# An attention-plus-MLP kernel on one core: the next item's first products ahead of the last item's third and fourth

## The chip, the cores and the metric

The kernel runs on one core of a Trainium2 chip. Time is device microseconds (us) of one execution; lower is better. The kernel before ran three times for its time and once more under the profiler. Engines are named as in the profile: PE (TensorE matmul), PEld (its weight load), DVE (VectorE), ACT (ScalarE), POOL (GpSimd), SP (SyncE).

## The reference

```
def _attn_ref(q, k, v, tau):                  # q, k, v: (2, 6016, 256)
    qn = q / (np.linalg.norm(q, axis=1, keepdims=True) + 1e-06)
    kn = k / (np.linalg.norm(k, axis=1, keepdims=True) + 1e-06)
    s = kn.transpose(0, 2, 1) @ qn / tau      # 256 x 256 per batch
    s = s - s.max(-1, keepdims=True)
    a = np.exp(s)
    a /= a.sum(-1, keepdims=True) + 1e-09
    return v @ a
def _moe_ref(x, w_in, w_out, alpha):          # x: (12032, 256), w_in: 256 x 2048
    h = x @ w_in
    g = np.maximum(h, 0.0) + alpha * np.minimum(h, 0.0)
    return g @ w_out
```

## The kernel before

The attention matrix is small, so the kernel folds it into the first weight: M = a @ w_in per batch. What is left per token is g = prelu(v @ M) and out = g @ w_out. The 12032 tokens are cut into 24 tiles of 500 or 504 tokens, twelve per batch, and the 2048 hidden units into eight pairs of 256. One tile and one pair make an *item*; item i has tile t = i // 8 and pair j = i % 8, and there are 192. Every float32 product is made in three passes of split operands (high by high, high by low, low by high), so one "product" below is three PE instructions at lines L115 to L117.

The first layer of an item is done with seven half-width products and additions between them (a Strassen-Winograd scheme). `pe_a` makes two products into the PSUM tile `q` (tag in the trace: q), which ACT copies out in `copies` (L605 into r0, L606 into p7). `pe_b` adds two products onto r0. `add_p7(i, 0)` on DVE (L622) makes the first half of r1 from r0 and p7. `pe_c` adds the third and fourth products, one onto that half of r1 and one onto r0. `add_p7(i, 1)` (L622 again) makes the other half of r1, and only then may `pe_d` add the last product onto r0. The activation takes two steps for each half: `act_n` on ACT (L635) and `dve_g` on DVE (L644), for r1 (n = 1) first, then r0 (n = 0).

The second layer has two forms. In most tiles, and for odd j in all of them, `g_high` (ACT, L653) and `g_low` (DVE, L657) split g, and twelve full-width products follow. In tiles 13 to 22 (`S_TILES`), even j is done by a second Strassen-Winograd scheme: `g_sums` (DVE, L694 to L699) makes sums t of g; `x_high` (ACT, L704) and `x_low` (DVE, L708) split g, `t_low` (ACT L717 and a POOL transfer L718) and `t_high` (ACT, L722) split t. Their products go to four PSUM banks X; `s2_first` runs three iterations after the item began and `s2_second` four. When a tile is through, `combine` (ACT L786, DVE L787 to L793) and two `finish_out` (DVE L800, then a transfer) empty the banks. `s_weights` makes four sets of summed weights on POOL (L680 to L686) with one ACT cast (L685) in each.

Each engine works through its own queue in the order in which the code issues. The order is written out by hand in one loop, `for i in range(NI + LAG)`: in iteration i the first layer of item i begins (`pe_a`, `pe_b`), that of item i-1 ends (`pe_c`, `pe_d`, activation), item i-2 is split, and the second layer of items i-3 and i-4 runs. At an iteration's end stands side work from a table (`side`): the preparation of the next tile's v in `v_sums`, `v_high`, `v_low` by the numbers `when`, and `s_weights`. `early` and `late` hold the two `finish_out` and `combine`: `combine` at the end of the iteration with j = 2, `finish_out` in the one with j = 3.

From tile 12 on r1 has one PSUM buffer (`r1_tile(..., alone=True)`), r0 has two, q has one.

Of the kernel before, what the change touches and what calls it, by code (L numbers as in the profile page):

```python
# [25 lines left out]
def fused_kernel(  # L26
# [67 lines left out]
    def f32(ap):  # L94
        return ap.bitcast(F32)
# [3 lines left out]
    def r1_tile(shape, name, alone=False):  # L99
        if alone or r1_at[0] % 2 == 0:  # L100
            r1_at[0] = 1
            return ps_r1.tile(shape, F32, tag="r1", name=name)
        r1_at[0] = 0
        return ps_x.tile(shape, F32, tag="x", name=name)
# [475 lines left out]
    def half_of(i):  # L580
        return tiles[items[i][0]][2] // 2

    def prod(out, i, p, first):
        t, j = items[i]
        h = half_of(i)
        m, v = M[tiles[t][0], j], v_spl[t]
        passes(
            out[:, :h], m[:, 0, p], m[:, 1, p], v[:, 0, p, :h], v[:, 1, p, :h],
            first, True, shared=True,
        )  # L590
# [6 lines left out]
    def copies(i):  # L597
        h = half_of(i)
        x = q_t.pop(i)
        r_t[i] = [  # L600
            ps_r.tile([P, 2, HW_], F32, tag="r0", name=f"r0_{i}"),
            r1_tile([P, 2, HW_], f"r1_{i}", alone=items[i][0] >= S_TILES[0] - 1),
        ]
        p7_t[i] = p7pool.tile([P, HW_], F32, tag="p7", name=f"p7_{i}")
        nc.scalar.copy(r_t[i][0][:, :, :h], x[:, 0:1, :h].broadcast_to([P, 2, h]))  # L605
        nc.scalar.copy(p7_t[i][:, :h], x[:, 1, :h])  # L606

    def pe_b(i):
        prod(r_t[i][0][:, 0], i, 1, False)
        prod(r_t[i][0][:, 1], i, 5, False)  # L610

    def pe_c(i):
        prod(r_t[i][1][:, 0], i, 3, False)
        prod(r_t[i][0][:, 1], i, 4, False)

    def pe_d(i):
        prod(r_t[i][0][:, 1], i, 2, False)

    def add_p7(i, n):
        h = half_of(i)  # L620
        r = r_t[i]
        nc.vector.tensor_tensor(  # L622
            out=r[1][:, n, :h], in0=r[0][:, 1, :h], in1=p7_t[i][:, :h], op=ALU.add
        )

    def blocks(x, i, a, b):
        h = half_of(i)
        return x[:, a * h : b * h].rearrange("p (n c) -> p n c", n=b - a)
# [11 lines left out]
    def dve_g(i, fi):  # L640

        f = 2 * items[i][1] + fi
        g = blocks(g_t[i], i, 2 * fi, 2 * fi + 2)
        nc.vector.scalar_tensor_tensor(  # L644
            out=g, in0=r_t[i][fi][:, :, : half_of(i)], scalar=sgn[:, f : f + 1],
            in1=g, op0=ALU.mult, op1=ALU.max,
        )

    def g_high(i, fi):
        w = tiles[items[i][0]][2]  # L650
        if fi == 1:
            gs_t[i] = [gpool.tile([P, 2, TW], F32R, tag=x, name=f"{x}{i}") for x in ("gh", "gl")]
        nc.scalar.copy(gs_t[i][0][:, fi, :w], g_t[i][:, fi * w : fi * w + w])  # L653

    def g_low(i, fi):
        w = tiles[items[i][0]][2]
        nc.vector.tensor_tensor(  # L657
            out=gs_t[i][1][:, fi, :w], in0=g_t[i][:, fi * w : fi * w + w],
            in1=f32(gs_t[i][0][:, fi, :w]), op=ALU.subtract,
        )  # L660
# [5 lines left out]
    def in_s(i):  # L666
        return 0 <= i < NI and items[i][0] in S_TILES

    def is_s(i):
        return in_s(i) and items[i][1] in S_J  # L670
# [30 lines left out]
    def x_high(i):  # L701
        h = half_of(i)
        xs_t[i] = [raw.tile([P, 2 * TW], F32R, tag="raw", name=f"{x}{i}") for x in ("xh", "xl")]
        nc.scalar.copy(xs_t[i][0][:, h : 4 * h], g_t[i][:, h : 4 * h])  # L704
# [8 lines left out]
    def t_low(i):  # L713

        w = 4 * half_of(i)
        ts_t[i] = [gpool.tile([P, 2 * TW], F32R, tag=x, name=f"t{x}{i}") for x in ("gh", "gl")]
        nc.scalar.activation(ts_t[i][1][:, :w], tt_t[i][:, :w], AF.Copy, scale=-1.0)  # L717
        nc.gpsimd.dma_start(out=ts_t[i][1][:, :w], in_=tt_t[i][:, :w], accum_op=ALU.add)  # L718
# [87 lines left out]
    def stage2(i):  # L806

        t, j = items[i]
        b, t0, w = tiles[t]
        if j == 0:  # L810
            po_t[t] = [ps_o.tile([P, TW], F32, tag=f"o{m}", name=f"o{m}_{t}") for m in range(NM)]
        gh, gl = gs_t.pop(i)
        todo = []

        end = i == NI - 1
        h = w // 2
        for c0, c1 in ((0, h), (h, w)) if end else ((0, w),):
            for m in range(NM):
                ms = slice(m * P, m * P + P)
                for fi in (1, 0):  # L820
                    f = 2 * j + fi
                    wh, wl = wo[:, 0, f, ms], wo[:, 1, f, ms]
                    for n, (x, y) in enumerate(((wh, gh), (wh, gl), (wl, gh))):
                        first = j == 0 and fi == 1 and n == 0
                        last = j == NPAIR - 1 and fi == 0 and n == 2
                        todo.append((m, c0, c1, x, y[:, fi, c0:c1], first, last))
        shared = t == len(tiles) - 1
        for n, (m, c0, c1, x, y, first, last) in enumerate(todo):
            o = po_t[t][m][:, c0:c1]
            nc.tensor.matmul(o, x, y, start=first, stop=last or shared, skip_group_check=shared)  # L830
            if last:
                if m == 0 and c0 == 0:
                    ob_t[t] = opool.tile([P, NM, TW], F32, tag="ob", name=f"ob{t}")
                nc.scalar.copy(ob_t[t][:, m, c0:c1], o)
                nc.sync.dma_start(
                    out=outT.rearrange("(m p) b n -> p m b n", p=P)[:, m, b, t0 + c0 : t0 + c1],
                    in_=ob_t[t][:, m, c0:c1],
                )
            if n in (4, len(todo) - 1):
                yield  # L840


    with tc.manual_schedule():
# [24 lines left out]
        for x in mix:  # L868
# [7 lines left out]
            else:  # L876
                f = load_wi if x == "i" else load_wo
# [90 lines left out]
        last0 = (per_b - 1) * NPAIR  # L968
        side = {}

        def at_item(i, f, *args):
            side.setdefault(i, []).append((f, args))
# [6 lines left out]
        i = NPAIR + 4  # L979
# [16 lines left out]
        i = (i + 2 * len(pieces) + NPAIR - 1) // NPAIR * NPAIR + 4  # L996
# [5 lines left out]
        for j in range(NPAIR):  # L1002

            i = last0 + 2 + 11 * j // 7
# [5 lines left out]
            ))  # L1010
            at_item(i + 1, lambda j=j: m_split(a1, j))
        for n in range(len(S_J)):
            at_item(last0 + 14 + n, s_weights, n)
        early, late = {}, {}
        for t in S_TILES:
            i = (t + 1) * NPAIR - 1 + LAG
# [2 lines left out]
            late[i + 1] = [lambda t=t: finish_out(t, 1)]  # L1019
        for t in range(1, len(tiles)):  # L1020

            when = (1, 1, 2, 2, 3, 4, 5, 6) if t > 1 else (4, 4, 4, 5, 5, 6, 7, 7)
            steps = (
                (v_sums, 0), (v_sums, 1), (v_high, 1), (v_high, 2),
                (v_high, 0), (v_low, 0), (v_low, 1), (v_low, 2),
            )
            for i, (f, part) in zip(when, steps):
                at_item((t - 1) * NPAIR + i, f, t, part)
# [14 lines left out]
        for i in range(NI + LAG):  # L1043


            new, one, two = i < NI, 0 <= i - 1 < NI, 0 <= i - 2 < NI
            s2 = stage2(i - LAG) if i >= LAG and not in_s(i - LAG) else None
            s_two = two and is_s(i - 2)
            if one:
                pe_c(i - 1)  # L1050
                add_p7(i - 1, 1)
            for f in early.get(i, []):
                f()
            if s_two:
                x_high(i - 2)
                g_sums(i - 2)
            elif two:
                g_high(i - 2, 1)
                g_high(i - 2, 0)
            if new:  # L1060
                pe_a(i)
                copies(i)
            if s_two:
                x_low(i - 2)
                t_low(i - 2)
            elif two:
                g_low(i - 2, 1)
                g_low(i - 2, 0)
            if in_s(i - LAG - 1):
                s2_second(i - LAG - 1)  # L1070
            if s2 or i < LAG:
                pe_s2(s2)
            if one:
                act_n(i - 1, 1)
                dve_g(i - 1, 1)
                pe_d(i - 1)
            if new:
                pe_b(i)
                add_p7(i, 0)
            if one:  # L1080
                act_n(i - 1, 0)
                dve_g(i - 1, 0)
            if s_two:
                t_high(i - 2)
            for f, args in side.get(i, []):
                f(*args)
            if in_s(i - LAG):
                s2_first(i - LAG)
            else:
                pe_s2(s2)  # L1090
            for f in late.get(i, []):
                f()
            if i == LAG:

                pe_fill()
# [32 lines left out]
```

## Time and profile before

| what | value |
|---|---|
| time, three runs | median 1154.54 us (1154.49 to 1155.5) |
| profiled execution, its own time | 1154.63 us |
| its span (first to last instruction) | 1152.9 us |
| PE busy | 1115.6 us, 97% |
| DVE busy | 914.8 us, 79% |
| ACT busy | 843.2 us, 73% |
| POOL busy | 91.9 us, 8% |

PE's busy time is modelled: matmuls overlap, each instruction's record is longer than its share of the engine's time, so a short stop between two of them does not show as idle. How far apart two instructions *start* says more. A row of the timeline gives start, length, engine, line, and in brackets the idle time before it and what ended it.

### The profile page before, as it was taken

The numbers are of one execution on the slowest core, as the hardware profiler recorded it, in microseconds if no ns is written. First come the engines' busy times: TensorE is split into PE (matmuls) and PEld (weight loads), VectorE is DVE, ScalarE is ACT, GpSimd is POOL, SyncE is SP. The second block draws the span as 40 slices with busy tenths as digits, with TensorE's granted clock in tenths as the row PEclk, the third lists the DMA queues.
The fourth block names the chain that finished last, engine by engine and source line by source line (L and its number), as shares of the span: only waits on it lengthen the run. The fifth ranks groups of instructions, "written<-read, shape, count | busy, mean of one in ns | idle before, by whom it ended". The sixth has DMA issues, their size and how long they took to land.

```text
span 1152.9 us, 19204 instructions
## 1 busy us (share of the span) xinstructions
PE 1115.6 (97%) x7284; PEld 1009.5 (88%) x7284; DVE 914.8 (79%) x1693; ACT 843.2 (73%) x1498; POOL 91.9 (8%) x118
## 2 busy tenths in 40 slices
PE   9999999999999999999999989999999999999998
PEld 8888999999999998999998878888888888889887
DVE  6798876777777777778788988788888888887875
ACT  6788677777778767767777677777777777777765
POOL 0000000000000000000002511011011011010100
PEclk9999999999999999999999999999999999999999
DMA  9996123232233101101101043333343342442410
GB/s 336 358 333 232 36 73 90 73 107 76 80 97 89 37 19 54 36 19 54 37 19 37 19 104 78 73 90 81 76 96 62 82 107 44 101 90 55 89 36 19
DMA packets 54589, 103.59 MB, mean 90 GB/s; under 512 B 5088, under 2 KB 30944, under 8 KB 54496
## 3 DMA queue, kind: packets, MB, share of 16 engines
q1 hardware_dynamic: 36224, 70.01, 18.2%
q0 software_dynamic: 18272, 32.34, 14.0%
q8 instruction: 58, 0.95, 0.3%
q14 instruction: 35, 0.29, 0.1%
HBM read 57.68 MB, written 12.32 MB: 61 GB/s over the span
## 4 chain that ended last, share of the span: by engine, by line
PE 69%; DVE 19%; issue 5%; ACT 5%; POOL 1%; DMA 0%; SPq 0%; DVEq 0%; ACTq 0%; POOLq 0%
PE o L830 24%; PE r L115 8%; PE r L117 7%; PE r L116 7%; PE S L401 7%; DVE g L644 5%; DVE r L622 4%; PE q L116 3%; PE q L117 3%; PE q L115 3%; ACT g L635 3%; DVE t L694 2%; PE X L115 2%; PE X L117 2%; PE X L116 2%
## 5 line engine op out<-in xcount | busy, mean ns | idle before, releaser
L644 DVE SCALAR_TENSOR_TENSOR g<-r,sgn,g 128x500 f32<-128x500 f32 (+1 forms) x384 | 282.1, 735 | 99.8 <-ACT g L635 99.5
L115 PE MATMUL r<-vs,m 128*128 128x250 f32 (+1 forms) x960 | 275.1, 287 | 31.1 <-DVE r L622 30.5
L830 PE MATMUL o<-gh,wo 128*128 128x500 f32 (+2 forms) x904 | 296.4, 389 | 1.5 <-DVE ob L800 1.5
L635 ACT ACTIVATE g<-r,salpha 128x500 f32<-128x500 f32 (+1 forms) x384 | 257.7, 683 | 29.2 <-PE r L117 16.8
L117 PE MATMUL r<-vs,m 128*128 128x250 f32 (+1 forms) x960 | 268.1, 279 | 0.0
L116 PE MATMUL r<-vs,m 128*128 128x250 f32 (+1 forms) x960 | 268.0, 279 | 0.0
L622 DVE TENSOR_TENSOR r<-r,p 128x250 f32<-128x250 f32 (+1 forms) x384 | 163.2, 425 | 102.4 <-PE r L117 94.6
L115 PEld LDWEIGHTS r<-vs,m 128*128 128x128 f32 x960 | 180.8, 188 | 65.1 <-DVE r L622 53.7
L605 ACT COPY r<-q 128x500 f32<-128x500 f32 (+1 forms) x192 | 108.1, 563 | 142.5 <-PE q L117 142.4
L657 DVE TENSOR_TENSOR gl<-g,gh 128x500 fp32r<-128x500 f32 (+1 forms) x304 | 196.6, 688 | 0.7 <-ACT gh L653 0.4
L653 ACT CAST gh<-g 128x500 fp32r<-128x500 f32 (+1 forms) x304 | 178.8, 613 | 22.1 <-DVE g L644 21.3
L116 PEld LDWEIGHTS r<-vs,m 128*128 128x128 f32 x960 | 181.4, 189 | 9.9
L830 PEld LDWEIGHTS o<-gh,wo 128*128 128x128 f32 x904 | 162.1, 188 | 24.6 <-DVE ob L800 1.8
L117 PEld LDWEIGHTS r<-vs,m 128*128 128x128 f32 x960 | 181.5, 189 | 0.0
L830 PE MATMUL o<-gl,wo 128*128 128x500 f32 (+2 forms) x452 | 175.3, 388 | 0.0
L115 PE MATMUL q<-vs,m 128*128 128x250 f32 (+1 forms) x384 | 107.4, 280 | 0.0
L116 PE MATMUL q<-vs,m 128*128 128x250 f32 (+1 forms) x384 | 107.3, 279 | 0.0
L117 PE MATMUL q<-vs,m 128*128 128x250 f32 (+1 forms) x384 | 107.2, 279 | 0.0
L830 PEld LDWEIGHTS o<-gl,wo 128*128 128x128 f32 x452 | 84.8, 188 | 13.7
L341 POOL DMA_DIRECT2D vs<-vt x46 | 36.1, 848 | 597.5 <-PE q L117 383.8
L401 PE MATMUL S<-kq 128*128 128x256 f32 x332 | 74.7, 379 | 0.0
L116 PEld LDWEIGHTS q<-vs,m 128*128 128x128 f32 x384 | 72.5, 189 | 0.1
(144 smaller groups left out, 1750.6 us busy)
## 6 DMA issues: line engine op xcount, KB each, us to landing
tgl<-t POOLq DMA_DIRECT2D x28, 500.0 KB, 4.6
kqT<-kqT_dram SPq DMA_DIRECT2D x20, 512.0 KB, 3.7
kq<-k_dram SPq DMA_DIRECT2D x39, 256.0 KB, 5.4
kq<-q_dram SPq DMA_DIRECT2D x39, 256.0 KB, 5.4
v<-vT_dram SPq DMA_DIRECT2D x16, 500.0 KB, 3.8
vs<-vt POOLq DMA_DIRECT2D x32, 250.0 KB, 3.5
outT_dram<-ob SPq DMA_DIRECT2D x30, 250.0 KB, 2.2
tgl<-t POOLq DMA_DIRECT2D x12, 504.0 KB, 4.6
```

Source lines behind the costliest of these rows:

```text
L115: nc.tensor.matmul(out, wh, xh, start=first, stop=False, **s)
L116: nc.tensor.matmul(out, wh, xl, start=False, stop=False, **s)
L117: nc.tensor.matmul(out, wl, xh, start=False, stop=last, **s)
L341: nc.gpsimd.dma_start(out=v_spl[t][:, 0, sl, :h], in_=x)
L401: nc.tensor.matmul(self.S[cc], t[:, 0, j, cc * P : cc * P + P], t[:, 1, j, :], start=ci == 0 and j == 0 and not (self.shared and cc), stop ...
L605: nc.scalar.copy(r_t[i][0][:, :, :h], x[:, 0:1, :h].broadcast_to([P, 2, h]))
L622: nc.vector.tensor_tensor(out=r[1][:, n, :h], in0=r[0][:, 1, :h], in1=p7_t[i][:, :h], op=ALU.add)
L635: nc.scalar.activation(blocks(g_t[i], i, 2 * fi, 2 * fi + 2), r_t[i][fi][:, :, : half_of(i)], AF.Copy, scale=salpha[:, f : f + 1],)
L644: nc.vector.scalar_tensor_tensor(out=g, in0=r_t[i][fi][:, :, : half_of(i)], scalar=sgn[:, f : f + 1], in1=g, op0=ALU.mult, op1=ALU.max,)
L653: nc.scalar.copy(gs_t[i][0][:, fi, :w], g_t[i][:, fi * w : fi * w + w])
L657: nc.vector.tensor_tensor(out=gs_t[i][1][:, fi, :w], in0=g_t[i][:, fi * w : fi * w + w], in1=f32(gs_t[i][0][:, fi, :w]), op=ALU.subtract,)
L830: nc.tensor.matmul(o, x, y, start=first, stop=last or shared, skip_group_check=shared)
```

## The change

Five edits, all of order. `pe_c(i-1)` and `add_p7(i-1, 1)` move from the head of the iteration to behind `pe_a(i)` and `copies(i)`. For S items `g_sums` thereby comes ahead of `add_p7(i-1, 1)` on DVE; for the others `g_low(i-2, 1)` is issued ahead of it and `g_low(i-2, 0)` behind it. `finish_out(t, 0)` and `t_low` move from the first half of the iteration to behind `act_n(i-1, 1)` and `dve_g(i-1, 1)`. The preparation of the next tile's v starts an iteration or so earlier (`when`). The four `s_weights` stand in iterations 102, 104, 107 and 109 of the loop in place of 102 to 105.

```
-            at_item(last0 + 14 + n, s_weights, n)
+            at_item(last0 + (14, 16, 19, 21)[n], s_weights, n)
...
-            when = (1, 1, 2, 2, 3, 4, 5, 6) if t > 1 else (4, 4, 4, 5, 5, 6, 7, 7)
+            when = (0, 1, 1, 1, 2, 4, 5, 6) if t > 1 else (4, 4, 4, 5, 5, 6, 7, 7)
             steps = (
                 (v_sums, 0), (v_sums, 1), (v_high, 1), (v_high, 2),
                 (v_high, 0), (v_low, 0), (v_low, 1), (v_low, 2),
...
-            if one:
-                pe_c(i - 1)
-                add_p7(i - 1, 1)
-            for f in early.get(i, []):
-                f()
             if s_two:
                 x_high(i - 2)
                 g_sums(i - 2)
             elif two:
                 g_high(i - 2, 1)
                 g_high(i - 2, 0)
+                g_low(i - 2, 1)
             if new:
                 pe_a(i)
                 copies(i)
+            if one:
+                pe_c(i - 1)
+                add_p7(i - 1, 1)
             if s_two:
                 x_low(i - 2)
-                t_low(i - 2)
             elif two:
-                g_low(i - 2, 1)
                 g_low(i - 2, 0)
...
             if one:
                 act_n(i - 1, 1)
                 dve_g(i - 1, 1)
+            for f in early.get(i, []):
+                f()
+            if s_two:
+                t_low(i - 2)
+            if one:
                 pe_d(i - 1)
```

On PE, at the head of iteration 140 (tile 17, j = 4), the program before has the last of `pe_c(139)` (r0_139), then `pe_a(140)` (q140), then `s2_second` (X3):

```order
L116 MATMUL r0_139_9122<-vs17_8505,m1_3_6316 128x250
L117 MATMUL r0_139_9122<-vs17_8505,m1_3_6316 128x250
L115 MATMUL q140_9179<-vs17_8505,m1_4_6445 128x250
L116 MATMUL q140_9179<-vs17_8505,m1_4_6445 128x250
L117 MATMUL q140_9179<-vs17_8505,m1_4_6445 128x250
L115 MATMUL q140_9179<-vs17_8505,m1_4_6445 128x250
L116 MATMUL q140_9179<-vs17_8505,m1_4_6445 128x250
L117 MATMUL q140_9179<-vs17_8505,m1_4_6445 128x250
L115 MATMUL X3_17_9196<-tgh136_9056,ws_6803 128x250
```

On PE at the same place the changed program has:

```order
L116 MATMUL q140_9172<-vs17_8453,m1_4_6449 128x250
L117 MATMUL q140_9172<-vs17_8453,m1_4_6449 128x250
L115 MATMUL r1_139_9116<-vs17_8453,m1_3_6316 128x250
L116 MATMUL r1_139_9116<-vs17_8453,m1_3_6316 128x250
L117 MATMUL r1_139_9116<-vs17_8453,m1_3_6316 128x250
L115 MATMUL r0_139_9115<-vs17_8453,m1_3_6316 128x250
L116 MATMUL r0_139_9115<-vs17_8453,m1_3_6316 128x250
L117 MATMUL r0_139_9115<-vs17_8453,m1_3_6316 128x250
L115 MATMUL X3_17_9192<-tgh136_9073,ws_6803 128x250
```

The six products of q now stand between the end of iteration 139 and the six that need `add_p7(139, 0)`.

On DVE, the end of a tile: before, from `combine` of tile 16 (c16) through iteration 139 (j = 3) to the sums t138 of iteration 140; the rows at L622 are `add_p7`, ob16 is `finish_out`:

```order
L787 TENSOR_TENSOR c16_9096<-X2_16_8649,c16_9096 128x250
L788 TENSOR_TENSOR c16_9096<-X3_16_8686,c16_9096 128x500
L793 TENSOR_TENSOR c16_9096<-X3_16_8686,c16_9096 128x250
L622 TENSOR_TENSOR r1_138_9051<-r0_138_9050,p7_138_9052 128x250
L800 TENSOR_TENSOR ob16_9108<-X0_16_8642,c16_9096 128x500
L657 TENSOR_TENSOR gl137_9112<-g137_9072,gh137_9111 128x500 x2
L644 SCALAR_TENSOR_TENSOR g138_9135<-r1_138_9051,sgn_108,g138_9135 128x500
L622 TENSOR_TENSOR r1_139_9123<-r0_139_9122,p7_139_9124 128x250
L644 SCALAR_TENSOR_TENSOR g138_9135<-r0_138_9050,sgn_108,g138_9135 128x500
L800 TENSOR_TENSOR ob16_9108<-X1_16_8696,c16_9096 128x500
L622 TENSOR_TENSOR r1_139_9123<-r0_139_9122,p7_139_9124 128x250
L694 TENSOR_TENSOR t138_9175<-g138_9135 128x500
```

On DVE at the same place the changed program has:

```order
L787 TENSOR_TENSOR c16_9098<-X2_16_8649,c16_9098 128x250
L788 TENSOR_TENSOR c16_9098<-X3_16_8682,c16_9098 128x500
L793 TENSOR_TENSOR c16_9098<-X3_16_8682,c16_9098 128x250
L657 TENSOR_TENSOR gl137_9104<-g137_9070,gh137_9103 128x500
L622 TENSOR_TENSOR r1_138_9046<-r0_138_9045,p7_138_9047 128x250
L657 TENSOR_TENSOR gl137_9104<-g137_9070,gh137_9103 128x500
L644 SCALAR_TENSOR_TENSOR g138_9134<-r1_138_9046,sgn_108,g138_9134 128x500
L800 TENSOR_TENSOR ob16_9137<-X0_16_8642,c16_9098 128x500
L622 TENSOR_TENSOR r1_139_9116<-r0_139_9115,p7_139_9117 128x250
L644 SCALAR_TENSOR_TENSOR g138_9134<-r0_138_9045,sgn_108,g138_9134 128x500
L800 TENSOR_TENSOR ob16_9137<-X1_16_8692,c16_9098 128x500
L694 TENSOR_TENSOR t138_9168<-g138_9134 128x500
```

A `g_low` now stands ahead of `add_p7(138, 1)`, the first `finish_out` stands behind `dve_g(138, 1)`, and `add_p7(139, 1)` has gone behind the sums.

On ACT, iteration 138 (j = 2) of the changed program, from the first activation of item 137 to `g_high`; vs18 is `v_high(18, 0)`, c16 the copy of `combine`:

```order
L635 ACTIVATE g137_9070<-r1_137_8985,salpha_109 128x500
L717 ACTIVATE tgl136_9074<-t136_9034 128x1000
L635 ACTIVATE g137_9070<-r0_137_8984,salpha_109 128x500
L722 CAST tgh136_9073<-t136_9034 128x1000
L343 CAST vs18_8963<-v18_8718 128x250
L343 CAST vs18_8963<-v18_8718 128x2x250
L786 COPY c16_9098<-X2_16_8649 128x250
L653 CAST gh137_9103<-g137_9070 128x500 x2
```

Before, L717 stood ahead of both L635, and the two casts of vs18 came one iteration later, so that L722 was followed by L786 at once.

## Rows read from the trace of the kernel before

**Rows 1.** The page: its head.
```profile
span 1152.9 us, 19204 instructions
```

**Rows 2.** Waits of PE, whole span: line, releaser, total us, times, longest.
```profile
PE r L115 <- DVE r L622: 30.5, 57, 1.6
PE o L830 <- DVE ob L800: 1.5, 1, 1.5
```

**Rows 3.** Waits of PE, 120 to 600 us.
```profile
PE r L115 <- DVE r L622: 0.8, 1, 0.8
```

**Rows 4.** Timeline of PE, two items of tile 18, 907 to 918 us.
```profile
907.28 0.28 PE L115 MATMUL q<-vs,m 128*128 128x250 f32 x1
...
909.40 0.28 PE L115 MATMUL r<-vs,m 128*128 128x250 f32 x1
...
910.45 0.39 PE L115 MATMUL X<-gh,wo 128*128 128x500 f32 x1
...
911.59 0.39 PE L117 MATMUL X<-gh,wo 128*128 128x500 f32 x1
912.49 0.38 PE L115 MATMUL r<-vs,m 128*128 128x250 f32 x1 [0.51 <-DVE r L622]
912.71 0.28 PE L116 MATMUL r<-vs,m 128*128 128x250 f32 x1
...
917.46 0.28 PE L115 MATMUL r<-vs,m 128*128 128x250 f32 x1
```

**Rows 5.** Timeline of DVE, the same two items.
```profile
907.91 0.68 DVE L694 TENSOR_TENSOR t<-g 128x500 f32<-128x500 f32 x1
...
909.41 0.93 DVE L708 TENSOR_TENSOR xl<-g,xh 128x750 fp32r<-128x750 f32 x1
911.17 0.74 DVE L644 SCALAR_TENSOR_TENSOR g<-r,sgn,g 128x500 f32<-128x500 f32 x1 [0.82 <-ACT g L635]
912.01 0.43 DVE L622 TENSOR_TENSOR r<-r,p 128x250 f32<-128x250 f32 x1
912.35 0.73 DVE L644 SCALAR_TENSOR_TENSOR g<-r,sgn,g 128x500 f32<-128x500 f32 x1
```

**Rows 6.** Timeline of ACT, the same two items.
```profile
909.53 1.04 ACT L717 ACTIVATE tgl<-t 128x1000 fp32r<-128x1000 f32 x1 [0.50 <-DVE t L699]
910.48 1.23 ACT L635 ACTIVATE g<-r,salpha 128x500 f32<-128x500 f32 x2
```

**Rows 7.** Timeline of PE: the same place (j = 3) in tiles 18 and 19.
```profile
890.23 0.38 PE L115 MATMUL r<-vs,m 128*128 128x250 f32 x1 [1.09 <-DVE r L622]
...
934.72 0.38 PE L115 MATMUL r<-vs,m 128*128 128x250 f32 x1 [1.07 <-DVE r L622]
```

**Rows 8.** Timeline of DVE, the end of tile 17, 890 to 895 us.
```profile
890.73 0.41 DVE L787 TENSOR_TENSOR c<-X,c 128x250 f32<-128x250 f32 x1
...
892.55 0.67 DVE L800 TENSOR_TENSOR ob<-X,c 128x500 f32<-128x500 f32 x1
893.13 1.26 DVE L657 TENSOR_TENSOR gl<-g,gh 128x500 fp32r<-128x500 f32 x2
```

**Rows 9.** Timeline of ACT, the end of tile 17.
```profile
889.33 1.02 ACT L722 CAST tgh<-t 128x1000 fp32r<-128x1000 f32 x1
890.25 0.38 ACT L786 COPY c<-X 128x250 f32<-128x250 f32 x1
890.51 1.14 ACT L653 CAST gh<-g 128x500 fp32r<-128x500 f32 x2
...
894.29 0.90 ACT L343 CAST vs<-v 128x250 fp32r<-128x250 f32 x2
```

**Rows 10.** Waits of PE, 643 to 676 us.
```profile
PE r L115 <- DVE r L622: 3.4, 6, 1.6
```

**Rows 11.** Timeline of DVE, 649.6 to 653.4 us.
```profile
650.53 2.82 DVE L657 TENSOR_TENSOR gl<-g,gh 128x504 fp32r<-128x504 f32 x2
```

**Rows 12.** Timeline of POOL, the same stretch.
```profile
651.08 1.73 POOL L680 TENSOR_TENSOR sw<-wo 128x512 f32<-128x512 f32 x1
```

More of the change, by code (lines that the diff above doesn't have):

```diff
@@ L1012, in fused_kernel @@
         for n in range(len(S_J)):
-            at_item(last0 + 14 + n, s_weights, n)
+            at_item(last0 + (14, 16, 19, 21)[n], s_weights, n)
         early, late = {}, {}
@@ L1020, in fused_kernel @@
         for t in range(1, len(tiles)):
-            when = (1, 1, 2, 2, 3, 4, 5, 6) if t > 1 else (4, 4, 4, 5, 5, 6, 7, 7)
+            when = (0, 1, 1, 1, 2, 4, 5, 6) if t > 1 else (4, 4, 4, 5, 5, 6, 7, 7)
             steps = (
@@ L1048, in fused_kernel @@
             s_two = two and is_s(i - 2)
[L1049 to L1053, printed above, removed]
             if s_two:
@@ L1059, in fused_kernel @@
                 g_high(i - 2, 0)
+                g_low(i - 2, 1)
             if new:
@@ L1062, in fused_kernel @@
                 copies(i)
+            if one:
+                pe_c(i - 1)
+                add_p7(i - 1, 1)
             if s_two:
                 x_low(i - 2)
-                t_low(i - 2)
             elif two:
-                g_low(i - 2, 1)
                 g_low(i - 2, 0)
@@ L1075, in fused_kernel @@
                 dve_g(i - 1, 1)
+            for f in early.get(i, []):
+                f()
+            if s_two:
+                t_low(i - 2)
+            if one:
                 pe_d(i - 1)
```

## The prediction, written before the changed kernel ran

> **What bounds the kernel now.** The head of the page gives the span, 1152.9 us [rows 1]; PE is busy for 97% of it. So I went to the view of waits for PE first: nearly all of its idle time has one cause, 57 waits of the third product (L115, in `pe_c` or `pe_d`) for an `add_p7` on DVE [rows 2]. The same view by stretches says where: between 120 and 600 us there is one such wait [rows 3], so the plain tiles have no loss to give back, and the rest lies in tiles 12 to 22. The timeline of PE shows what a wait costs. In the stretch of two items, 18 half-width products start between 907.28 and 909.40, one every 0.118 us, and full-width ones every 0.228 (five from 910.45 to 911.59). The next should have started at 911.82 and started at 912.49; the one after it came 0.22 later and not 0.118 [rows 4]. So a wait shown as 0.51 costs 0.67 + 0.10 us: the idle figure plus 0.26.
>
> Now a whole tile. By these paces an S item (even j) issues `pe_a` 0.71, `pe_c` 0.71, `s2_second` 1.41, `pe_d` and `pe_b` 1.05, the first half of an ordinary item 1.37: 5.25 us. An odd one issues 0.71 + 0.71 + 1.37 + 1.05 + 1.06 = 4.9 (the row: 912.49 to 917.46, with 0.1 of restart in it [rows 4]; I take 4.86). Four pairs are 40.4 us. The same place of two successive tiles lies 44.49 us apart [rows 7], so **a tile loses 4.1 us**. Of the ten S tiles, nine (14 to 22) are of this kind; tile 13 has the weight sums in it.
>
> Why PE waits there: the timeline of DVE shows `dve_g` idle for 0.82 us until `act_n` on ACT was done, then `add_p7` at 912.01 to 912.44, and PE starts at 912.49 [rows 5, 4]. The timeline of ACT shows why `act_n` was late: `t_low` (1.04 us) stood ahead of it and waited for the sums [rows 6].
>
> **The ordinary pair after the change.** No arithmetic is added or removed; only waits can move. I lay out an even item from the start of `pe_a` = 0. The odd item before it ends with nine small products, so `pe_b`'s results are there at 0.88 before 0 (0.16 of tail on the last product), `add_p7` runs 0.43, `dve_g` starts 0.34 after it and takes 0.73 [rows 5]: it ends at +0.2. `g_sums` takes 1.50 (907.91 to 909.41 [rows 5]), to 1.75; `add_p7(1)` then ends at 2.2. Its input from `pe_c` is there at 1.58, and `pe_d` wants it at 0.71 + 0.71 + 1.41 = 2.83: **0.6 us to spare**. `x_low` (0.93) ends near 3.0; `act_n(1)` runs 2.2 to 2.9, since `t_low` now stands behind it; `dve_g(1)` 3.0 to 3.7; `add_p7(0)` starts when `pe_b`'s results come, 4.05, and ends at 4.5. `pe_c` wants it at 5.25 + 0.71 = 5.96, after the next `pe_a`: 1.4 us to spare. The odd item, by the same steps with `g_low` 0.6 each, has 0.7 and 1.1 to spare. So ordinary pairs lose nothing; the wait is gone, not moved.
>
> **The end of a tile**, once in each of tiles 14 to 22. Here I find new waits. With j = 1, `v_sums(1)` (two dependent subtractions, 0.8) lies before `g_sums`; `add_p7(1)` ends at 2.9 in place of 2.2, and PE loses about 0.2 in j = 2. There ACT goes on from `act_n(1)` (to 3.6) through `t_low` and `act_n(0)` (0.95 and 0.57 more [rows 6]) and `t_high` (0.92 from start to start [rows 9]) to 6.0. Then come two casts of `v_high(0)`, one iteration earlier than before and now ahead of `combine`: 0.90 as a pair [rows 9], 0.8 on the queue. The copy L786 ends at 7.05. `combine` on DVE takes 1.5 (890.73 to 892.55 less one `add_p7` of 0.33 [rows 8]), to 8.65; `g_low` 0.6; `add_p7(1)` ends at 9.6. The odd item j = 3 began at 5.45, and its `pe_d` wants that sum at 8.23: a wait of 1.4. Behind it stand `act_n(1)` 0.7, `dve_g(1)` 0.7 and `finish_out(t, 0)` 0.67 [rows 8], which ends at 11.65 because it has been put behind `dve_g`; the first product into its bank is wanted at 10.8: another 0.9. With 0.1 of restart each, **a tile end costs 0.2 + 1.5 + 1.0 = 2.7 us**, where all waits of a tile cost 4.1 before. Gain 1.4 a tile, 9 tiles: **12.6 us**. Bounds: the second wait would be nothing if DVE ran some other work in less time than laid out (1.7 a tile), and each of four steps could be 0.2 later (3.5): 5 to 22 us.
>
> **The weight sums.** Between 643 and 676 us PE waits six times for `add_p7`, 3.4 us idle [rows 10], which is 5 us with 0.26 each. Two of DVE's casts take 2.82 us there [rows 11] while POOL adds [rows 12], where two take 1.26 elsewhere [rows 8]: 1.56 us of DVE time for a set of sums. Spread over twice the time, sets 1 to 3 each meet an item with some 1 us of slack, so part of the stall stays. I take 3.5 of 5 as gained (bounds 0 and 5). [...]
>
> **Losses.** (1) In plain tiles `add_p7(1)` comes later by 0.7 of `pe_a` and 0.6 of a `g_low`, while `pe_d` stays. Its slack there falls from 1.2 to 0.5. In most items nothing happens. Going through the DVE timeline, I find eight iterations (at the start, with the second batch's norms, and with its M) in which side work fills DVE until shortly before `pe_d`; each would lose 0.1 to 0.6, in sum 3.4 (bounds 0 and 5). (2) `pe_a(103)` now asks for the last part of M 0.7 us sooner than it was ready by: 0.7. (3) At the end of tile 22, the first matmul of the plain tile 23 waits for `finish_out(22, 0)`, now behind `dve_g`: 1.8 more, beside the existing wait of 1.5 for the other bank [rows 2].
>
> Sum: -12.6 - 3.5 + 3.4 + 0.7 + 1.8 = -10.2 us on a span of 1152.9 and an execution of 1154.63, which is 0.09 above the median of the runs. From 1154.5 that gives **1144 us**, its own range 1136 to 1152.
>
> **The rivals.** About 0.2% (2.3 us) is what a measurement of this kernel can tell from no change.
>
> *The tile end is hidden too.* If ACT and DVE have caught up by j = 3, only about 1 us a tile is lost: 9 x 1.7 = 15 more, 1129. For it: DVE is idle for a fifth of the time. Against: the queues are in order, and idle time in other items doesn't help.
>
> *The weight sums gain nothing*, since the two engines block each other wherever the sums stand: 3.5 less, 1148. Rows 11 and 12 show the blocking; against it, before, four sets stood in four items in a row. [...]
>
> *Slower: `pe_d` waits in every S item.* `g_sums` and its 1.5 us now stand ahead of the sum that `pe_d` needs. The price is what `add_p7(1)` lacks beyond 0.6 us of slack. There are 27 ordinary pairs in these nine tiles; the gain of 10.2 is used up at 0.38 a pair, so at a lateness of 0.9 us in all. At 1.4 us it would be 0.8 + 0.1 each, 24 in sum: 1168. For it: that DVE chain has no gaps. Against: each of its links has a row, and the slack is over a third of the chain.
>
> *No change.* A tile end that costs 3.7 us and not 2.7 takes 9 us back: 1153. For it: each link there adds to the next, and nothing in the queue can absorb it.
>
> **How the numbers follow.** Forecast 0.52, weight sums without gain 0.15, tile end hidden 0.13, no change 0.09, slower 0.11. Faster by over 0.2% are the first three: 0.80; within it 0.09; slower 0.11. The range runs from 1132, which leaves out the far half of the hidden case, to 1154, which leaves out the slower case.
>
> **What would show it.** Right: in tiles 14 to 22 `dve_g` no longer idles for `act_n` in ordinary pairs; PE waits for `add_p7` fall from five a tile to about two, both at j = 3, one of over 1 us at `pe_d` and one at the first X product for L800; the same place in successive tiles lies 43.1 us apart; DVE, ACT and PE are busy as long as before, but for POOL's blocking. Wrong: a wait at `pe_d` in j = 4, 6 and 0; a wait of PE for ACT's copies L605; a tile period under 42 or over 44; or waits in plain tiles beyond eight.

## The result, and the profile after

The changed kernel takes 1160.73 us (median of seven runs, 1157.22 to 1163.18), the kernel before 1154.54 (1154.47 to 1155.5). The ratio is 1.0054, 95% interval 1.004 to 1.0068: **slower by half a per cent**, where 1144 us was forecast, with a chance of 0.11 for slower. The runs of the changed kernel lie further apart than those of the kernel before; the reason is found below. The profiled execution is the one of 1163.18 us.

The head of its page, which answers to [rows 1], with its `dve_g` row, and then that row in the page of before:

```profile
span 1161.4 us, 19221 instructions
PE 1122.4 (97%) x7284; PEld 1022.3 (88%) x7284; DVE 921.3 (79%) x1693; ACT 843.5 (73%) x1498; POOL 92.8 (8%) x118
L644 DVE SCALAR_TENSOR_TENSOR g<-r,sgn,g 128x500 f32<-128x500 f32 (+1 forms) x384 | 282.8, 736 | 36.8 <-ACT g L635 36.7
```

```profile
L644 DVE SCALAR_TENSOR_TENSOR g<-r,sgn,g 128x500 f32<-128x500 f32 (+1 forms) x384 | 282.1, 735 | 99.8 <-ACT g L635 99.5
```

The idle time of `dve_g` behind `act_n` falls from 99.5 to 36.7 us. The waits of PE over the whole span, which answer to [rows 2], are fewer:

```profile
PE r L115 <- DVE r L622: 22.7, 24, 2.2
PE X L115 <- DVE ob L800: 7.4, 9, 0.8
PE o L830 <- DVE ob L800: 3.0, 2, 1.5
```

Together these are 33.1 us of idle time in 35 waits, where [rows 2] has 32.0 in 58: fewer waits, but no shorter in sum, since the ends of the tiles took over. To see where the 8.5 us of span went, I cut it at the first product of `pe_a` in tiles 12, 14 and 23. These are the rows of PE's timeline, of the kernel before and then of the changed one:

```profile
600.89 0.28 PE L115 MATMUL q<-vs,m 128*128 128x252 f32 x1
...
695.69 0.28 PE L115 MATMUL q<-vs,m 128*128 128x252 f32 x1
...
1095.73 0.28 PE L115 MATMUL q<-vs,m 128*128 128x250 f32 x1
```

```profile
607.61 0.28 PE L115 MATMUL q<-vs,m 128*128 128x252 f32 x1
...
702.36 0.28 PE L115 MATMUL q<-vs,m 128*128 128x252 f32 x1
...
1102.58 0.28 PE L115 MATMUL q<-vs,m 128*128 128x250 f32 x1
```

| stretch | before | after | difference | forecast |
|---|---|---|---|---|
| to tile 12 (plain) | 600.89 | 607.61 | +6.7 | +3.4 |
| tiles 12 and 13 (M of the second batch, weight sums) | 94.80 | 94.75 | -0.05 | +0.7 - 3.5 |
| tiles 14 to 22 (S tiles) | 400.04 | 400.22 | +0.2 | -12.6 |
| from tile 23 | 57.2 | 58.8 | +1.6 | +1.8 |

**The S tiles.** Ordinary pairs run as laid out: in tile 18 the items start 5.24 and 4.86 us apart, and PE does not wait in them (`dve_g` still idles there for `act_n`, 0.23 to 0.27 us where it was 0.82). The end of a tile is another matter. Here is PE at j = 3 of tile 19, first products behind each wait and the pace that follows:

```profile
944.93 0.39 PE L115 MATMUL r<-vs,m 128*128 128x250 f32 x1 [1.35 <-DVE r L622]
...
947.06 0.58 PE L115 MATMUL X<-xh,wo 128*128 128x250 f32 x1 [0.81 <-DVE ob L800]
947.44 0.42 PE L116 MATMUL X<-xl,wo 128*128 128x250 f32 x1
947.65 0.41 PE L117 MATMUL X<-xh,wo 128*128 128x250 f32 x1
...
950.26 0.28 PE L115 MATMUL r<-vs,m 128*128 128x250 f32 x1
950.38 0.28 PE L116 MATMUL r<-vs,m 128*128 128x250 f32 x1
```

Both waits are there, at the two places forecast, with 1.35 and 0.81 us of idle time. With the 0.26 that a wait costs beside its idle figure [rows 4] they are 1.61 and 1.07, where 1.5 and 1.0 were laid out. But behind the second the same 250-column products start 0.21 us apart and not 0.12, for 3.4 us. The view of windows shows why. Its columns are the stretch and its length, busy time and count of PE, PEld, DVE, ACT and POOL, the granted clock, DMA's share and GB/s:

```profile
946.70:950.00 3.30, 2.94 (x13) 2.94 (x14) 3.23 (x7) 0.82 (x1) 0.00 (x0) 0.50 0.38 142
950.10:953.40 3.30, 3.30 (x30) 3.30 (x30) 1.97 (x3) 2.56 (x5) 0.00 (x0) 1.00 0.01 2
```

The granted clock is 0.50, and then 1.00 again. The fall begins at 946.63, inside the second wait, and lasts 3.41 us. The same place one tile later, in PE's timeline and in the windows:

```profile
989.54 0.38 PE L115 MATMUL r<-vs,m 128*128 128x250 f32 x1 [1.34 <-DVE r L622]
...
991.67 0.38 PE L115 MATMUL X<-xh,wo 128*128 128x250 f32 x1 [0.81 <-DVE ob L800]
991.90 0.27 PE L116 MATMUL X<-xl,wo 128*128 128x250 f32 x1
992.01 0.28 PE L117 MATMUL X<-xh,wo 128*128 128x250 f32 x1
```

```profile
991.20:994.50 3.30, 2.83 (x24) 2.83 (x25) 3.23 (x7) 1.59 (x3) 0.00 (x0) 1.00 0.35 130
```

The waits are the same and the clock stays. So it goes in the profiled execution: in seven of nine tiles (14, 15, 17, 18, 19, 21, 22) the clock is 0.50 for 3.41 us there, and they take 44.6 to 45.0 us; in tiles 16 and 20 it is not, and they take 43.28 and 43.26 (43.1 was forecast). In tile 18, j = 3 and j = 4 take 8.49 + 5.82, in tile 16 7.56 + 5.22: **a fall costs 1.5 us, seven of them 10.8**. The kernel before has waits of up to 1.09 there [rows 7], one at a time, and its clock is 1.00. The other runs fit: the run of 1157.22 us had a mean clock of 0.994, that of 1163.18 0.990, and the other five 0.990 or 0.991. By these means, at 3.41 us each, the clock fell four times in the first, seven in the second and six or seven in the others (an estimate); without 1.5 us for each fall all seven runs would lie between 1151 and 1153. What differs between executions is mainly how often the clock falls.

**The plain tiles.** In tiles 2 to 7, which lost nothing before, j = 3 now takes 5.7 to 5.83 us and not 5.2. ACT from the end of j = 2 of tile 6 on, then DVE and PE at its j = 3:

```profile
362.07 1.05 ACT L419 ACTIVATE kqT<-kqT 128x1024 f32<-128x1024 f32 x1
363.02 0.19 ACT L419 ACTIVATION_READ_ACCUMULATOR kqT<-kqT 128x1 f32 x1
363.11 0.90 ACT L343 CAST vs<-v 128x250 fp32r<-128x250 f32 x2
363.91 1.05 ACT L834 COPY ob<-o 128x500 f32<-128x500 f32 x2
364.85 1.13 ACT L653 CAST gh<-g 128x500 fp32r<-128x500 f32 x2
```

```profile
365.50 0.68 DVE L657 TENSOR_TENSOR gl<-g,gh 128x500 fp32r<-128x500 f32 x1 [2.30 <-ACT gh L653]
366.10 0.42 DVE L622 TENSOR_TENSOR r<-r,p 128x250 f32<-128x250 f32 x1
```

```profile
366.57 0.38 PE L115 MATMUL r<-vs,m 128*128 128x250 f32 x1 [0.34 <-DVE r L622]
```

L419 squares a piece of the second batch's k and q, L834 empties the last tile's banks, L343 is `v_high(0)`, an iteration earlier than before. ACT reaches `g_high` (L653) late; `g_low` on DVE waits 2.30 us for it, and `add_p7(1)`, which the change has put behind this `g_low`, waits with it though its own inputs are there (the last product of `pe_c` ends at 365.09). In tiles 1 and 8 to 10 no L419 stands there; the same early `v_high(0)` costs nothing in them, and j = 3 takes 5.2 us.

### The profile page after: what moved, and what is told of

It reads as the page before. It is cut to its first block, busy times and chain, and to the rows that moved or that the text cites. A ratio compares the mean times of both kernels' runs of the same rounds, so it can differ in the third digit from the quotient of the medians.

```text
span 1161.4 us, 19221 instructions
## 1 busy us (share of the span) xinstructions
PE 1122.4 (97%) x7284; PEld 1022.3 (88%) x7284; DVE 921.3 (79%) x1693; ACT 843.5 (73%) x1498; POOL 92.8 (8%) x118
## 4 chain that ended last, share of the span: by engine, by line
PE 79%; DVE 11%; ACT 7%; issue 2%; DMA 0%; SPq 0%; ACTq 0%; DVEq 0%
PE o L830 23%; PE r L115 8%; PE r L117 8%; PE r L116 8%; PE S L401 6%; PE X L115 5%; PE X L117 4%; PE X L116 4%; PE q L116 3%; PE q L115 3%; PE q L117 3%; ACT g L635 2%; DVE r L622 2%; DVE gl L657 2%; DVE g L644 1%
## 5 line engine op out<-in xcount | busy, mean ns | idle before, releaser
L635 ACT ACTIVATE g<-r,salpha 128x500 f32<-128x500 f32 (+1 forms) x384 | 260.6, 680 | 137.4 <-DVE r L622 82.1
L644 DVE SCALAR_TENSOR_TENSOR g<-r,sgn,g 128x500 f32<-128x500 f32 (+1 forms) x384 | 282.8, 736 | 36.8 <-ACT g L635 36.7
L622 DVE TENSOR_TENSOR r<-r,p 128x250 f32<-128x250 f32 (+1 forms) x384 | 163.2, 425 | 128.5 <-PE r L117 125.0
L657 DVE TENSOR_TENSOR gl<-g,gh 128x500 fp32r<-128x500 f32 (+1 forms) x304 | 206.1, 678 | 27.9 <-ACT gh L653 26.5
L653 ACT CAST gh<-g 128x500 fp32r<-128x500 f32 (+1 forms) x304 | 177.0, 612 | 32.1 <-DVE g L644 31.0
L115 PE MATMUL q<-vs,m 128*128 128x250 f32 (+1 forms) x384 | 110.1, 287 | 0.0
L116 PE MATMUL q<-vs,m 128*128 128x250 f32 (+1 forms) x384 | 109.1, 284 | 0.6 <-DVE vs L349 0.6
L117 PE MATMUL q<-vs,m 128*128 128x250 f32 (+1 forms) x384 | 108.9, 284 | 0.3 <-DVE m L111 0.3
L341 POOL DMA_DIRECT2D vs<-vt x46 | 33.6, 733 | 669.7 <-PE q L117 393.2
L116 PEld LDWEIGHTS q<-vs,m 128*128 128x128 f32 x384 | 74.7, 194 | 6.9 <-DVE vs L349 0.9
L115 PEld LDWEIGHTS q<-vs,m 128*128 128x128 f32 x384 | 74.3, 194 | 6.1
```

The source lines that it names most:

```text
L115: nc.tensor.matmul(out, wh, xh, start=first, stop=False, **s)
L116: nc.tensor.matmul(out, wh, xl, start=False, stop=False, **s)
L117: nc.tensor.matmul(out, wl, xh, start=False, stop=last, **s)
L341: nc.gpsimd.dma_start(out=v_spl[t][:, 0, sl, :h], in_=x)
L622: nc.vector.tensor_tensor(out=r[1][:, n, :h], in0=r[0][:, 1, :h], in1=p7_t[i][:, :h], op=ALU.add)
L635: nc.scalar.activation(blocks(g_t[i], i, 2 * fi, 2 * fi + 2), r_t[i][fi][:, :, : half_of(i)], AF.Copy, scale=salpha[:, f : f + 1],)
```

## The experiments

Each kernel is the changed one with the edit shown, unless it says otherwise. Beside all of them ran the kernel before (medians 1154.37, 1154.42 and 1154.82 us in the three groups of runs).

**1. `v_high(0)` back by one iteration.**

```
-            when = (0, 1, 1, 1, 2, 4, 5, 6) if t > 1 else ...
+            when = (0, 1, 1, 1, 3, 4, 5, 6) if t > 1 else ...
```

> The changed kernel with one number put back: v_high(0) in the iteration with j = 3, as before, not j = 2. Theory 1 (the two casts of v_high, ahead of the copies and casts that follow on ACT, cause both new losses): the plain tiles 2 to 7 go back from 42.3 to 41.65 us (3.5 us in all), the wait at pe_d in j = 3 of the S tiles falls from 1.5 to about 0.7 us, and if the granted clock then stays at 1.00 the seven losses of 1.5 us go too: 1160.7 - 3.5 - 7 - 10.5 = 1140 us; 1150 if the clock still falls. Rival (pe_a ahead of pe_c is what costs): no change, 1158 to 1162.

Measured: **1140.01 us**, ratio 0.9873 (0.9858 to 0.9888), the clock 1.00 at all tile ends. Tiles 2 to 7 take 41.46 to 41.7 again, and tile 12 starts at 603.51. At the end of a tile the changed kernel's ACT and DVE read:

```profile
940.23 1.03 ACT L722 CAST tgh<-t 128x1000 fp32r<-128x1000 f32 x1
941.15 0.91 ACT L343 CAST vs<-v 128x250 fp32r<-128x250 f32 x2
941.96 0.37 ACT L786 COPY c<-X 128x250 f32<-128x250 f32 x1
```

```profile
942.37 0.42 DVE L787 TENSOR_TENSOR c<-X,c 128x250 f32<-128x250 f32 x1 [1.25 <-ACT c L786]
```

In this kernel, ACT and PE at the same place:

```profile
924.99 1.03 ACT L722 CAST tgh<-t 128x1000 fp32r<-128x1000 f32 x1
925.90 0.38 ACT L786 COPY c<-X 128x250 f32<-128x250 f32 x1
```

```profile
928.88 0.38 PE L115 MATMUL r<-vs,m 128*128 128x250 f32 x1 [0.53 <-DVE r L622]
...
931.01 0.38 PE L115 MATMUL X<-xh,wo 128*128 128x250 f32 x1 [0.82 <-DVE ob L800]
```

DVE idled 1.25 us for the copy of `combine` behind the two casts; now it comes right behind `t_high`, the first wait is 0.53 in place of 1.35, and with waits of 0.53 and 0.82 the clock stays at 1.00. One digit in one table turns the slower kernel into a faster one.

**2. The first `finish_out` back**, to where it stands behind `add_p7(i-1, 1)` and ahead of `dve_g`.

```
                 add_p7(i - 1, 1)
+            for f in early.get(i, []):
+                f()
...
                 dve_g(i - 1, 1)
-            for f in early.get(i, []):
-                f()
```

> The changed kernel with finish_out(t, 0) put back to right behind add_p7(i-1, 1). Theory 1: the wait of the first X product for L800 in j = 3 (0.8 us idle, 1.0 in all) goes in nine tiles, 9 us; the wait at pe_d stays at 1.5 us and so do the plain tiles' 0.6; with one wait in place of two the clock falls in fewer tiles or in none (0 to 10.5 us): 1141 to 1152. Rival (the second wait only moves on to the next add_p7, since DVE has the same work to do in the same iteration): 1158 to 1162.

Measured: **1146.47 us**, 0.9931 (0.9918 to 0.9943). The waits for L800 in S tiles are gone and the first wait stays; alone, it leaves the clock at 1.00 at every tile end. But the clock falls once in tile 13, in a single, longer wait at j = 3, with 3.41 us at 0.50 from 677.56:

```profile
677.71 0.58 PE L115 MATMUL r<-vs,m 128*128 128x252 f32 x1 [2.20 <-DVE r L622]
```

The changed kernel has a wait of 2.20 in that place too, and its clock stayed at 1.00 there. Tile 18 takes 42.64: j = 3 6.46, and j = 4 5.74 where 5.24 was laid out.

**3. Both back.**

> The changed kernel with both put back: v_high(0) at j = 3 and finish_out(t, 0) behind add_p7(i-1, 1). Theory 1: a tile end loses 0.2 + 0.8 us, a tile takes 41.4 us (44.5 before and in the changed kernel), the plain tiles 41.65, the clock stays at 1.00: 1160.7 - 3.5 - 28 = 1129 us. Rival (pe_a ahead of pe_c costs): 1155 or more.

Measured: **1133.54 us**, 0.9819 (0.9805 to 0.9832), 4.5 us above what I expected. The sum of the two edits' gains holds in j = 3 (5.67), but j = 4 loses half a microsecond (5.72) in each of nine tiles, as in experiment 2. The second `finish_out` (L800), at the end of j = 3, stands ahead of the sums of j = 4; DVE is back to back there:

```profile
970.70 0.67 DVE L800 TENSOR_TENSOR ob<-X,c 128x500 f32<-128x500 f32 x1
971.29 0.67 DVE L694 TENSOR_TENSOR t<-g 128x500 f32<-128x500 f32 x1
...
972.78 0.42 DVE L622 TENSOR_TENSOR r<-r,p 128x250 f32<-128x250 f32 x1
```

**4. Work for PE in the two waits.** Matmuls with a zero operand, added onto an X bank that keeps its value: ahead of `pe_d` and ahead of `s2_first` at j = 3 of each tile end, first six and four of them. They add zero and need nothing that is late (`zeros` is a tile set to 0 at the start of the kernel).

```
...
+        def pe_zero(i, n):
+            for _ in range(n):
+                nc.tensor.matmul(
+                    bank(items[i - LAG - 1][0], 1)[:, 0:256].rearrange("p (n c) -> p n c", n=8),
+                    ones, zeros.rearrange("p (n c) -> p n c", n=1).broadcast_to([P, 8, 32]),
+                    start=False, stop=True, skip_group_check=True,
+                )
...
+            if i in early:
+                pe_zero(i, 6)
             if one:
                 act_n(i - 1, 1)
...
             if in_s(i - LAG):
+                if i in early:
+                    pe_zero(i, 4)
                 s2_first(i - LAG)
```

> The changed kernel with all its waits, and with PE given work in them: six matmuls that add zero to a bank that is already full, ahead of pe_d in j = 3, and four ahead of the first X product there, 0.22 us each. The result is the same. Theory 1 (a low clock behind the waits costs some 1.5 us in seven tiles): the granted clock stays at 1.00, the waits stay as they were, 1160.7 - 10.5 = 1150 us. Rival (the low clock falls into time that PE waits anyway and costs nothing): 1160 to 1163, or more by the filling where it ends later than the wait.

Measured: 1170.08 us, 1.0135 (1.0121 to 1.0149). The clock is 1.00 at all nine ends (it falls once in tile 13, as in experiment 2), but each matmul left two records and took 0.43 us. So they overran the waits: `pe_d` starts 0.9 us later than in the changed kernel, the first X product another 0.65, and j = 3 takes 9.19. On the price it settles nothing.

**5. The same with three and two.**

> The changed kernel with half the filling: three matmuls that add zero ahead of pe_d in j = 3 and two ahead of the first X product, 0.43 us each by the trace of the longer filling, which overran the two waits by 1.1 and 0.7 us. Theory 1 (the low clock behind the waits costs 1.5 us in each tile where it falls): PE waits as long as in the changed kernel, the granted clock stays at 1.00 at all nine tile ends, j = 3 takes 7.6 and j = 4 5.2 us: 1149 to 1151. Rival (the low clock costs nothing that the waits don't cost): 1159 to 1163.

Measured: **1154.0 us**, 0.9996 (0.9987 to 1.0005). PE at the end of tile 19, and the window behind it:

```profile
937.51 1.46 PE L1041 MATMUL X<-zeros,ones 128*128 128x256 f32 x6
939.01 0.38 PE L116 MATMUL r<-vs,m 128*128 128x250 f32 x1
...
940.18 1.03 PE L1041 MATMUL X<-zeros,ones 128*128 128x256 f32 x4
941.14 0.38 PE L116 MATMUL X<-xh,wo 128*128 128x250 f32 x1
941.36 0.28 PE L117 MATMUL X<-xl,wo 128*128 128x250 f32 x1
```

```profile
940.60:943.90 3.30, 3.30 (x26) 2.95 (x25) 3.23 (x7) 1.52 (x3) 0.00 (x0) 1.00 0.31 121
```

The clock is 1.00 at all nine ends, j = 3 takes 7.56 and j = 4 5.21, and every tile is within 0.2 us of tiles 16 and 20 of the changed kernel: tiles 14 to 22 take 389.5 us in place of 400.2. Nothing that PE waits for came sooner: in tiles 19 and 20 `add_p7(1)` and the first `finish_out` end 4.22 and 6.35 us behind the start of j = 3, in both kernels to 0.02. In all eleven runs the mean clock is 0.998 or more, so it is not one lucky execution. The 10.8 us are thus the clock's, shown and not only read off. The time is 3 us over my expectation. Tile 23 has a filler too, where it costs 1.3; tile 13, where the clock fell once, took 0.7 longer; and I had taken the price of seven falls off the median, 1160.7, where the execution that had the seven took 1163.2.

**6. The new `when` alone, in the kernel before.**

> The kernel before with the new numbers of when alone (v_high(0) at j = 2 and the other steps earlier). Theory 1 (the two casts hurt because g_low now stands ahead of add_p7 on DVE, so in the old order they hurt the S tiles alone, through combine): plain tiles unchanged at 41.65 us, S tiles 0.5 to 1 us longer each: 1158 to 1163. Rival (an early v_high(0) hurts in any order): plain tiles 2 to 7 0.6 us longer too, 1162 to 1167. Third: it changes nothing in the old order, 1154.

Measured: 1156.01 us, 1.0013 (1.0004 to 1.0022), a smaller loss than I expected. S tiles take 44.5 to 44.7, 0.1 more than before; j = 3 of plain tiles loses 0.2. In the old order `add_p7(1)` stands ahead of both `g_low` and does not share their lateness: the early `v_high(0)` is dear only with the new order on DVE.

**7. The spread of the weight sums alone, in the kernel before.**

> The kernel before with the weight sums spread, alone. As predicted for the change: 3.5 us faster, 1151, from tiles 12 and 13. Rival (the two engines block each other wherever the sums stand): 1154 to 1155.

Measured: 1152.65 us, 0.9984 (0.9975 to 0.9993). Tile 13 falls from 45.70 to 44.04: 1.7 us of the 3.5 that I had in the sum.

**8. The loop's order alone** (`when` and `s_weights` as before).

> The edits of the loop alone: the changed kernel with when and the weight sums as they were before. Theory 1: it holds what the order gains (no wait in ordinary pairs) without the early v_high(0): 1139 to 1144, clock 1.00; tile 13 by some 2 us worse than with the sums spread. Rival (the earlier v_sums and the spread weight sums are needed for the new order): 1148 or more.

Measured: 1148.01 us, 0.9942 (0.993 to 0.9955), 4 us over my theory and at the 1148 of its rival, of which the earlier `v_sums` is borne out. The clock does not fall at the tile ends (waits of 0.53 and 0.81). S tiles take 43.1: j = 3 6.75, and j = 2 6.08 (5.43 in experiment 1), since the old `when` has its `v_sums` ahead of the sums there. The clock falls once, in tile 13, 0.9 us behind a single wait of 1.97, and j = 2 takes 9.0 there.

**9. Experiment 3, with the weight sums unspread** (the four sets in iterations 102 to 105).

```
-            at_item(last0 + (14, 16, 19, 21)[n], s_weights, n)
+            at_item(last0 + 14 + n, s_weights, n)
```

> Both of my steps undone, and the four sets of weight sums in four items in a row again. Theory: the spread gave 1.9 us in the old order and gives 2 to 3 in the new one: 1135.5 to 1137. Rival of the forecast (3.5 us, as I had it in the sum): 1137. Rival by blocking (it does not matter where the sums stand): 1133.5.

Measured: 1133.11 us, 0.9815 (0.9802 to 0.9829): nothing is lost without the spread; my theory falls, and the rival by blocking (1133.5) holds. Tile 13 takes 42.85 unspread and 43.32 spread. Unspread, the loss is in j = 2 (6.9); spread, in j = 5 and 6 (6.27 and 6.01 us). The DVE sums of an S item beside POOL's last step of a set, in this kernel's timelines of DVE and POOL (the same L694 takes 0.67 in the rows of experiment 3):

```profile
665.15 1.78 DVE L694 TENSOR_TENSOR t<-g 128x504 f32<-128x504 f32 x1
```

```profile
665.05 1.33 POOL L686 TENSOR_TENSOR ws<-sw,ws 128x512 fp32r<-128x512 f32 x1 [0.73 <-ACT ws L685]
```

**10. Experiment 3, with `combine` later**, behind `add_p7` of j = 3.

```
-            late[i] = [lambda t=t: combine(t)]
-            early[i + 1] = [lambda t=t: finish_out(t, 0)]
+            early[i + 1] = [lambda t=t: (combine(t), finish_out(t, 0))]
```

> Both of my steps undone, and combine (ACT copy 0.4 us, DVE 1.5 us) also moved, from the end of j = 2 to behind add_p7 of j = 3. Theory: the order on DVE decides which sum is late, and the work of combine must be passed through that queue in any case: pe_d of j = 3 no longer waits (0.4 us a tile back), but the sums of j = 4 come 1.5 us later and PE waits there instead; about 1132 to 1137 us, no gain over 1133.5. Rival: j = 3 has room for it on DVE, and nine tile ends give 0.4 to 0.7 us each: 1127 to 1130.

Measured: 1143.17 us, 0.99 (0.9887 to 0.9914). The wait moves, as my theory had it, but it is dearer than I laid out: the first X product waits for L800 again (nine times, up to 1.0 us), and j = 3 and j = 4 take 6.06 and 6.21 where experiment 3 has 5.67 and 5.72.

**11. Experiment 3, with the second `finish_out` later**, behind `add_p7` of j = 4 (for the last S tile it stays).

```
-            late[i + 1] = [lambda t=t: finish_out(t, 1)]
+            (early if t + 1 in S_TILES else late).setdefault(i + 1 + (t + 1 in S_TILES), []).append(
+                lambda t=t: finish_out(t, 1)
+            )
```

> Both of my steps undone, and finish_out(t, 1) (0.67 us of DVE) moved from the end of j = 3 to behind add_p7 of j = 4, so that it no longer stands ahead of the sums g_sums of j = 4 (but for the last S tile). Theory: the 0.5 us that j = 4 loses beyond its layout is this instruction; nine tile ends without it give 3 to 5 us: 1129 to 1131. Rival: the first product into that bank, the last of s2_second in j = 4, then waits for L800 by about as much: 1133 to 1135.

Measured: 1137.64 us, 0.9853 (0.984 to 0.9866). The rival held, and more: j = 4 takes 6.2 in place of 5.72, since PE now waits for that bank:

```profile
933.90 0.38 PE L115 MATMUL X<-tgh,wo 128*128 128x250 f32 x1 [0.70 <-DVE ob L800]
```

By experiments 3, 10 and 11, DVE has no slack between j = 2 and j = 4: what is taken from ahead of one of its sums falls on the next thing that PE wants. Kernels 3 and 9 are the fastest found, some 21 us under the kernel before.

## Why the prediction was wrong

**Right.** That ordinary pairs lose nothing: they run at 5.24 and 4.86, and the slower rival (a wait of `pe_d` in every S item) did not come. The sign given for the forecast was too strong: `dve_g` still idles for `act_n` there, by a quarter of a microsecond, which costs PE nothing. That a tile end gets two new waits of PE, where they lie and how long they are: 2.9 us a tile where 2.7 was laid out, seen in tiles 16 and 20 and in all nine of experiment 5. That the first `finish_out` of tile 22 costs tile 23 1.8 us: its j = 3 goes from 8.33 to 10.11.

**The step that failed: "a tile end costs 0.2 + 1.5 + 1.0 = 2.7 us".** It takes the products behind each wait at 0.118 us, as they run behind the waits of the kernel before. Two waits of 1.35 and 0.81 us, with nine small products between them, brought the granted clock down to 0.50 for 3.41 us in seven of nine tiles, 1.5 us each. Of -12.6 us, 10.8 went to the clock and 2.0 to the tile end being 0.2 longer than laid out. I had not weighed a fall of the clock, because the kernel before, whose PE idles 2.7 us in an S tile in all where it is now 2.15, never shows one: its clock is 1.00 in every stretch up to 1150 us. Experiment 5 settles the price by giving PE work and nothing else: the clock is 1.00 at all nine ends, and tiles 14 to 22 take 389.5 us in place of 400.2; experiments 1, 2 and 8 show, at the tile ends, one wait of 1.35, or two of 0.53 and 0.8, without a fall. The clock fell at single waits as well: in tile 13 at one of 2.20 (experiments 2, 4 and 5) or 1.97 (experiment 8). Which tile ends are spared is not settled: tiles 19 and 20 have the same waits to 0.01 us.

**Plain tiles: +3.4 forecast, +6.7 measured.** Experiment 1 parts it: without the early `v_high(0)` it is 2.6, so the eight iterations that I summed come to no more than I had for them. The other 4.1 (3.4 in tiles 2 to 7, the rest in tile 11) I had at nothing: I followed `v_high(0)` at the ends of S tiles only. In tiles 2 to 7 ACT's slack was used up by L419 and L834, and DVE's queue hands the lateness on to `add_p7(1)`. Experiment 6 shows that most of it takes both edits: 0.2 us a tile in the old order, 0.6 in the new.

**Weight sums: -3.5 forecast.** In the changed kernel tile 13 gained 1.5; alone in the old order the spread gave 1.7, and beside experiment 9 nothing (-0.4), so the 1.5 need not be the spread's. The sets met S items, which have no 1 us of slack. The rival, by which the sums gain nothing wherever they stand, held there, where the order leaves DVE no slack; in experiment 9 a DVE sum took 1.78 us beside POOL's L686, where the same L694 takes 0.67 in experiment 3. In the old order, where the spread gave 1.7, it did not hold.

**Tile 12** took 1.4 more: the 0.7 of `pe_a(103)`, measured 0.8 (j = 7 of tile 12 goes from 6.37 to 7.20), and 0.6 elsewhere in it that I had not seen.

Summed up: +6.7 - 0.05 + 0.2 + 1.6 = 8.5 us of span. Without the clock it would be -2.3, some 1152 us (an estimate): still 8 short of the forecast, and near no change. That part is the plain tiles, the weight sums and the 0.2 at each tile end.

## What to carry to other kernels

Before a wait is split in two, or a new one is accepted, ask what PE's clock does behind it: here each of seven falls cost 1.5 us beside the waits themselves. The clock fell in seven of nine tile ends with two waits of together 2.15 us, and at single waits of 2.20 and 1.97 in tile 13; at tile ends with one of 1.35 (experiment 2) it stayed at 1.00. When work moves earlier on a queue, follow it through every kind of iteration and not only the one in which the change matters, to the next engine's queue as well. And undo a change part by part: here one digit of one table stood between half a per cent slower and over one faster.

## What the runs showed of the hardware

At the tile ends the granted clock was 0.50 for 3.41 us each of seven times. PE had waited twice, 1.35 and 0.81 us, with 1.3 us of products between, and the fall began within 0.5 us of the end of the second wait, on either side of it. At single waits it fell elsewhere: in tile 13, in the same way, 0.15 us before the end of one of 2.20 us (experiment 2), and 0.9 us behind the end of one of 1.97 (experiment 8). Neither kind of wait always met a fall: the same program with the same waits met it in seven of nine tile ends in one execution, and did not meet it behind its own 2.20 in tile 13. By their mean clocks, the other executions had four to seven falls, and the runs spread over 6 us where the kernel before spreads over 1. With zero matmuls in the waits the clock was 1.00 at all nine tile ends (experiments 4 and 5), and three and two of them cost no time where they fitted the wait: j = 3 took 7.56 us, as in tile 16 of the changed kernel.
